# A kept value is joined into the last product's half bank before that product instead of after it, and the last step's stores use other queues

## The chip, the cores and the metric

The kernel runs on one core of a Trainium2 chip. The metric is the device time of one execution in microseconds; the kernel before takes 2274.68 us, the median of 3 runs (2274.32 to 2275.0).

Engines are named as in the profile: PE (TensorE; its weight loads are listed apart as PEld), DVE (VectorE), ACT (ScalarE), POOL (GpSimd) and SP (SyncE, which here only issues DMAs). PSUM is the memory that matmuls write to; it comes in banks of 512 fp32 columns on 128 partitions.

## What is computed

A causal depthwise convolution over the sequence, whose 7 taps are the softmax of a small weight table per head, and behind it a two-layer network without biases, all in fp32:

```python
# x: (8, 4096, 192), weight: (8, 7)
w = softmax(weight, axis=-1)
out = np.einsum('hk,bskhg->bshg', w, x_unf)     # 7 shifted copies of x, 24 channels a head
x = out.reshape(32768, 192)
h = x @ w_in                                    # (192, 2048)
g = h * (1.0 / (1.0 + np.exp(-1.702 * h)))
return g @ w_out                                # (2048, 192)
```

## The kernel before

**Tiling.** The work goes in 32 big steps (`N_BIG`) of 1024 tokens: 512 positions from each of two sequences. A step has a first half, `hidden` (called twice), which multiplies the convolved tokens by `w_in` and applies the activation, and a second half, `second`, which multiplies the result by `w_out` and stores the output. Both use fast matrix multiplication schemes that trade products for sums: the first on 21 products (`TERMS`), the second on 25 (`FORM_OF`). The first big step has its own code (`first_step`, `second_first`); `second` is called for steps 1 to 31. While a step runs, DVE, ACT and POOL also prepare the convolution of the step after the next.

**The second half.** Its order is written out by hand in the list `PLAN`, the same list for all 31 steps. Each entry is an operation:

- `main f s to first`: begin a product of weight form `f` with the sum `s` into value `to`; `first` tells whether it overwrites or adds to what is there.
- `go n`: issue `n` of the product's steps. A step is four matmuls of 128 rows by 32 columns side by side on the array, three for the main product (one for each 32 output columns) and one for a side product (`side f s to`), which goes to the last 32 partitions of another bank and is copied out by ACT (L1016) when it is complete. A main product is four steps.
- `join dst a op b`: `dst = a + b` or `a - b` on DVE (`add_up`: L391 for a plus, L393 for a minus), 96 partitions by 256 columns.
- `seed dst src sign`: an ACT copy (L1020), to keep a value or to put a start value into PSUM.
- `turn m n o src`: a DVE transpose (L908) of a finished value into the output tile `osbs`; `store n o`: its DMAs (L919).
- `sum`, `acc`, `tap`, `cross`: sums of the activated tokens on DVE or by an adding DMA from POOL, and pieces of the next step's convolution.

A value is named `p0` to `p5` or `k0` to `k11`. The `k` values lie in SBUF. The `p` values are halves of three PSUM banks:

```python
mains, sides = (bs[0], bx[0], by[0]), (bx[1], bs[1], by[1])
...
return mains[i // 2][0:n3, i % 2 * T : (i % 2 + 1) * T] if name[0] == "p" else kept(i)
```

So `p4` and `p5` are the two halves of the bank `by[0]`. The profile calls this bank "sums" in odd steps and "slot" in even ones, because the tiles change roles from step to step.

The part of the plan that the change touches (two stretches; between them stand products 4, 15 and 12):

```python
("join", "p2", "p4", "+", "k3"), ("main", 8, 8, "p1", 0, 0, 2), ("go", 1),
("join", "k8", "k9", "+", "k5"), ("tap",), ("go", 1), ("join", "k8", "k7", "-", "k8"),
("main", 4, 6, "p4", 0), ("go", 1), ("turn", 1, 0, 1, "k10"), ("go", 1),
...
("turn", 1, 0, 0, "k6"), ("store", 0, 0), ("main", 24, 19, "p5", 0), ("go", 2), ("final",),
("join", "k1", "p3", "-", "k3"), ("go", 1), ("join", "k2", "p2", "-", "k4"),
("turn", 0, 0, 1, "k1"), ("store", 0, 1), ("go", 1), ("turn", 0, 1, 1, "k2"), ("store", 1, 1),
("join", "k1", "p5", "+", "k5"), ("turn", 0, 1, 0, "k1"), ("join", "k8", "k8", "+", "k0"),
("turn", 1, 1, 0, "k8"), ("store", 1, 0),
```

Product 24 is the last of a step and adds into `p5`. After it, `p5 + k5` is put into `k1` and turned, and `k8 + k0` is put into `k8` and turned; `k0` is the last side product, which ACT copies out.

**Queues.** Every engine takes its instructions in the order in which the program issues them, and the waits between engines are semaphore counts that a framework puts in from the tiles that an instruction reads and writes. Stores of steps 1 to 30 go out on SP's queue once both halves of a sequence are turned (`out_store`, `stored`). In the last step each of the four quarters is stored as soon as it is turned, in three DMAs (one for each 64 output columns), which alternate between the queues of ACT and SP:

```python
queues = (nc.sync, nc.scalar) if o else (nc.scalar, nc.sync)
store(big, n, o, queues + queues[0:1])
```

Of the kernel before, what the change touches and what calls it, by code (L numbers as in the profile page):

```python
# [15 lines left out]
def kernel(  # L16
# [29 lines left out]
    nc = tc.nc  # L46
# [92 lines left out]
    def spot(i):  # L139

        if i >= SPOTS:
            return block(*divmod(i - SPOTS, NG))
        flat = osbs[:, i * BLK : (i + 1) * BLK] if i < 2 else room[:, ROOMS[i - 2], :]
        return flat.rearrange("p (k t) -> p k t", k=NG)
# [3 lines left out]
    def kept(i):  # L148

        if i < NG * len(KEPT):  # L150
            return room[0 : NC * Q, KEPT[i // NG], i % NG * T : (i % NG + 1) * T]
        return spot(KEPT_LATE)[0 : NC * Q, i % NG, :]
# [66 lines left out]
    def form(i):  # L219

        if i < WHOLE:
            return w_out_s[:, i // NG, i % NG * NG : (i % NG + 1) * NG, :]
        return w_form[:, i - WHOLE, :, :]
# [165 lines left out]
    def add_up(v, dst, a, op, b, eng=vec):  # L389
        if op == "+":  # L390
            eng.tensor_add(v(dst), v(a), v(b))  # L391
        elif op == "-":
            eng.tensor_sub(v(dst), v(a), v(b))  # L393
        elif op == "n":
            vec.scalar_tensor_tensor(
                out=v(dst), in0=v(a), scalar=-1.0, in1=v(b), op0=ALU.mult, op1=ALU.subtract
            )
        else:
            vec.tensor_scalar_mul(v(dst), v(a), -1.0)
# [164 lines left out]
    def cross_piece():  # L564
        if pieces:
            cross(*pieces.pop(0))
# [195 lines left out]
    def chunk_cols(c):  # L762
        return slice(c * Q, (c + 1) * Q)
# [136 lines left out]
    def blocks(t):  # L900
        return t.rearrange("p (j t) -> p j t", t=Q)

    def chunk(t, c):
        return t[c * Q : (c + 1) * Q]

    def turn(m, n, src, js):

        vec.transpose(osb[:, n, js, m * Q : (m + 1) * Q], src)  # L908


    def store(big, n, o=None, queues=(nc.sync,) * 3):
        p, c = divmod(big, CHUNKS)
        js = slice(0, TOK // Q) if o is None else slice(o * T // Q, (o + 1) * T // Q)
        t = c * TOK + js.start * Q
        rows = out_v[n, p, t : t + (js.stop - js.start) * Q, :].rearrange(
            "(j i) (c e) -> c i j e", i=Q, e=2 * Q
        )
        for c in range(NC):
            queues[c].dma_start(out=rows[c], in_=osb[c * Q : (c + 1) * Q, n, js, :])  # L919
# [27 lines left out]
        ("side", 7, 20, "k1"), ("go", 2), ("sum", 6, 6, "-", 17), ("main", 10, 14, "p0", 0), ("go", 2),  # L947
        ("seed", "k5", "p2", 1), ("tap",), ("cross",), ("join", "k10", "k10", "+", "k8"), ("go", 2),
        ("join", "p2", "p4", "+", "k3"), ("main", 8, 8, "p1", 0, 0, 2), ("go", 1),
        ("join", "k8", "k9", "+", "k5"), ("tap",), ("go", 1), ("join", "k8", "k7", "-", "k8"),  # L950
        ("main", 4, 6, "p4", 0), ("go", 1), ("turn", 1, 0, 1, "k10"), ("go", 1),
        ("join", "k3", "p1", "+", "k6"), ("go", 1), ("tap",), ("join", "k3", "p0", "-", "k3"), ("go", 1),
        ("join", "k6", "k0", "-", "p0"), ("side", 8, 5, "k0"), ("main", 15, 12, "p2", 0), ("go", 2),
# [3 lines left out]
        ("turn", 1, 0, 0, "k6"), ("store", 0, 0), ("main", 24, 19, "p5", 0), ("go", 2), ("final",),  # L957
        ("join", "k1", "p3", "-", "k3"), ("go", 1), ("join", "k2", "p2", "-", "k4"),
        ("turn", 0, 0, 1, "k1"), ("store", 0, 1), ("go", 1), ("turn", 0, 1, 1, "k2"), ("store", 1, 1),
        ("join", "k1", "p5", "+", "k5"), ("turn", 0, 1, 0, "k1"), ("join", "k8", "k8", "+", "k0"),  # L960
        ("turn", 1, 1, 0, "k8"), ("store", 1, 0),
    ]

    def sum_g(dst, a, op, b=None):

        if op == "acc":
            nc.gpsimd.dma_start(out=spot(dst), in_=spot(a), accum_op=ALU.add)  # L967
        else:
            add_up(spot, dst, a, op, b)

    SIDE_HALF = (0, 0, 1, 0, 1, 0, 1)

    def second(big, bx, by, bs, final, last):

        n3 = NC * Q
        mains, sides = (bs[0], bx[0], by[0]), (bx[1], bs[1], by[1])
        side, count = [], [0]
        now = {}  # L980
        stored = {0: 0, 1: 0}

        def value(name):
            i = int(name[1:])
            return mains[i // 2][0:n3, i % 2 * T : (i % 2 + 1) * T] if name[0] == "p" else kept(i)

        def product(f, s, k0=0, k1=NG):
            return [(form(FORM_OF[f])[:, k, :], spot(s)[:, k, :]) for k in range(k0, k1)]

        def one_matmul(dst, w, t, first, last):  # L990
            nc.tensor.matmul(dst, w, t, start=first, stop=last, skip_group_check=True)  # L991

        def begin_side(f, s, to, *ks):
            steps = product(f, s, *ks)
            for c in range(NC):
                turns, i = divmod(count[0], NC)
                h = SIDE_HALF[turns]
                count[0] += 1
                dst = sides[i][n3:, h * T : (h + 1) * T]
                for k, (w, t) in enumerate(steps):  # L1000
                    end = k == len(steps) - 1
                    side.append((dst, w[:, chunk_cols(c)], t, k == 0 and h == 0, end and chunk(value(to), c)))

        def begin_main(f, s, to, first, *ks):
            now.update(steps=product(f, s, *ks), to=value(to), first=bool(first))

        def go(n):
            for _ in range(n):
                w, t = now["steps"].pop(0)
                for c in range(NC):  # L1010
                    one_matmul(chunk(now["to"], c), w[:, chunk_cols(c)], t, now["first"], not now["steps"])
                now["first"] = False
                d, ws, ts, st, to = side.pop(0)
                one_matmul(d, ws, ts, st, to is not False)
                if to is not False:
                    act.copy(to, d)  # L1016

        def seed(dst, src, sign):
            if sign == 1:
                act.copy(value(dst), value(src))  # L1020
            else:
                act.mul(value(dst), value(src), -1.0)

        def out_turn(m, n, o, src):
            turn(m, n, blocks(value(src)), slice(o * T // Q, (o + 1) * T // Q))

        def out_store(n, o):
            if last:
                queues = (nc.sync, nc.scalar) if o else (nc.scalar, nc.sync)
                store(big, n, o, queues + queues[0:1])  # L1030
                return
            stored[n] += 1
            if stored[n] == 2:
                store(big, n)

        ops = dict(
            sum=sum_g, acc=lambda d, a: sum_g(d, a, "acc"), main=begin_main, side=begin_side, go=go, seed=seed,
            join=lambda d, a, op, b: add_up(value, d, a, op, b), turn=out_turn, store=out_store,
            tap=next_tap, cross=cross_piece, final=final,
        )  # L1040
        for item in PLAN:
            ops[item[0]](*item[1:])
        assert not side and not now["steps"] and count[0] == NC * len(SIDE_HALF)
        while pieces:
            cross_piece()
# [250 lines left out]
```

## Time and profile before

| | |
|---|---|
| median of 3 runs | 2274.68 us |
| the profiled execution | 2274.41 us |
| its span, first to last instruction | 2272.6 us |
| granted TensorE clock | 1.000 |
| PE busy | 2263.4 us |
| DVE busy | 1941.0 us |
| ACT busy | 1568.8 us |
| POOL busy | 847.0 us |

The span is what the trace covers; the 1.8 us between it and the execution's own time lie before the first and after the last instruction. Busy times are of one engine each and overlap. In a line of the timeline the first number is the start in us from the span's beginning, the second how long the instruction or the run of like instructions took; then come the engine, the line of the kernel, the operation, the tile written and those read, the shape, the count, and in brackets the idle time of that engine just before, with what ended it. A fp32 matmul is recorded as two passes, each with its weight load.

### The profile page before, as it was taken

How to read it: one execution, taken by the hardware profiler on the slowest of the kernel's cores; microseconds unless marked ns; L12 is line 12 of the kernel's file. 1: busy time of each engine (PE TensorE's matmuls, PEld its weight loads, DVE VectorE, ACT ScalarE, POOL GpSimd, SP SyncE). 2: the span in 40 equal slices, each digit the busy share in tenths (PEclk: the TensorE clock that was granted, in tenths of full speed). 3: DMA queues.
4: the chain of work that ended last, by engine and by line, in shares of the span. 5: the costliest groups of instructions: out<-in, count | busy, mean ns of one | idle time of the engine just before them, and what ended most of it. 6: DMA issues, size and time to landing. Idle time of an engine off the chain costs nothing.

```text
span 2272.6 us, 60950 instructions
## 1 busy us (share of the span) xinstructions
PE 2263.4 (100%) x25214; PEld 1214.9 (53%) x25214; DVE 1941.0 (85%) x2794; ACT 1568.8 (69%) x2972; POOL 847.0 (37%) x834
## 2 busy tenths in 40 slices
PE   9999999999999999999999999999999999999998
PEld 5475555555555555555555555555555555555556
DVE  8998888888888888888888888888888888888877
ACT  8866776667766667666677666776667766667754
POOL 1544443244442344433444324444244442344400
PEclk9999999999999999999999999999999999999999
DMA  9976656656566665666655675656666566664443
GB/s 205 155 146 127 127 111 126 137 122 131 116 126 129 123 139 114 116 126 134 134 120 109 126 144 121 131 112 127 132 126 136 112 124 126 129 139 86 88 99 71
DMA packets 269908, 284.20 MB, mean 125 GB/s; under 512 B 117952, under 2 KB 206016, under 8 KB 269632
## 3 DMA queue, kind: packets, MB, share of 16 engines
q0 software_dynamic: 57648, 150.69, 36.9%
q1 hardware_dynamic: 210336, 129.22, 25.2%
q8 instruction: 199, 3.26, 0.6%
q14 instruction: 77, 0.63, 0.1%
q10 hardware_dynamic: 1648, 0.39, 0.1%
HBM read 53.15 MB, written 25.17 MB: 34 GB/s over the span
## 4 chain that ended last, share of the span: by engine, by line
PE 99%; DVE 1%; ACT 0%; DMA 0%; issue 0%; SPq 0%; ACTq 0%; DVEq 0%
PE slot L616 35%; PE slot L991 33%; PE sums L616 16%; PE sums L991 13%; PE slot L822 2%; DMA xin<-in_x_dram 0%; DVE room L657 0%; DVE xt L473 0%; ACT conv_t L1096 0%; DVE conv_t L504 0%; SPq L99 0%; ACT conv_t L357 0%; DVE room L393 0%; ACT conv_t L356 0%; DVE g L391 0%
## 5 line engine op out<-in xcount | busy, mean ns | idle before, releaser
L616 PE MATMUL slot<-conv_t,w_in_s 64*128 64x512 f32 x3740 | 862.5, 591 | 0.3 <-DVE w_in_s L376 0.3
L991 PE MATMUL slot<-g,w_form 128*32 128x256 f32 x7024 | 710.8, 379 | 0.4 <-DVE room L657 0.4
L616 PEld LDWEIGHTS slot<-conv_t,w_in_s 64*128 64x128 f32 x3740 | 377.6, 187 | 423.9 <-issue 347.7
L393 DVE TENSOR_TENSOR g<-g 128x1024 f32<-128x1024 f32 x372 | 448.9, 1234 | 3.2
L991 PEld LDWEIGHTS slot<-g,w_form 128*32 128x32 f32 x7024 | 375.7, 110 | 118.1 <-DVE room L657 0.9
L616 PE MATMUL sums<-conv_t,w_in_s 64*128 64x512 f32 x1660 | 408.3, 589 | 0.3 <-DVE w_in_s L376 0.3
L1016 ACT COPY room<-slot 32x256 f32<-32x256 f32 x434 | 159.3, 367 | 310.3 <-PE slot L991 309.2
L642 ACT ACTIVATE g<-room 128x1024 f32<-128x1024 f32 x310 | 325.7, 1077 | 67.9 <-DVE room L657 67.9
L991 PE MATMUL sums<-g,w_form 128*32 128x256 f32 x2648 | 368.8, 379 | 0.0
L991 PE MATMUL slot<-g,w_out_s 128*32 128x256 f32 x4080 | 318.8, 380 | 0.0
L967 POOL DMA_DIRECT2D g<-g x124 | 106.2, 857 | 496.6 <-PE slot L991 156.8
L616 PEld LDWEIGHTS sums<-conv_t,w_in_s 64*128 64x128 f32 x1660 | 172.1, 187 | 184.9 <-issue 140.0
L518 POOL TENSOR_TENSOR conv_t<-conv_t,g 128x512 f32<-128x512 f32 x180 | 262.2, 1457 | 16.3 <-POOL conv_t L518 3.0
L530 POOL DMA_DIRECT2D g<-g x120 | 105.5, 879 | 422.5 <-PE sums L991 128.7
L653 ACT COPY room<-slot 128x512 f32<-128x512 f32 x434 | 231.4, 601 | 38.5 <-PE slot L616 38.4
L516 ACT ACTIVATE g<-xt,cw 128x512 f32<-128x512 f32 x360 | 248.5, 730 | 2.2
L991 PEld LDWEIGHTS slot<-g,w_out_s 128*32 128x32 f32 x4080 | 164.7, 110 | 128.5 <-ACT g L638 22.7
L638 ACT ACTIVATE g<-slot 128x512 f32<-128x512 f32 x334 | 180.8, 598 | 45.4 <-PE slot L616 24.8
L991 PEld LDWEIGHTS sums<-g,w_form 128*32 128x32 f32 x2648 | 177.9, 110 | 37.6
L504 DVE SCALAR_TENSOR_TENSOR conv_t<-xt,cw,conv_t 128x512 f32<-128x512 f32 (+1 forms) x198 | 192.0, 970 | 4.6
L393 POOL TENSOR_TENSOR conv_t<-conv_t 128x256 f32<-128x256 f32 x180 | 181.9, 1024 | 9.4
L1016 ACT COPY room<-sums 32x256 f32<-32x256 f32 x217 | 79.6, 367 | 145.0 <-PE sums L991 142.5
(205 smaller groups left out, 2909.5 us busy)
## 6 DMA issues: line engine op xcount, KB each, us to landing
g<-g POOLq DMA_DIRECT2D x124, 512.0 KB, 5.8
xin<-in_x_dram SPq DMA_DIRECT2D x240, 180.0 KB, 4.3
conv_t<-conv_t SPq DMA_DIRECT2D x180, 192.0 KB, 3.1
g<-g POOLq DMA_DIRECT2D x120, 256.0 KB, 3.8
out_dram<-osbs SPq DMA_DIRECT2D x186, 128.0 KB, 4.9
g<-room POOLq DMA_DIRECT2D x31, 512.0 KB, 5.3
conv_t<-g POOLq DMA_DIRECT2D x60, 256.0 KB, 4.8
g<-osbs POOLq DMA_DIRECT2D x30, 512.0 KB, 4.7
```

What stands on the lines that cost most here:

```text
L393: eng.tensor_sub(v(dst), v(a), v(b))
L504: vec.scalar_tensor_tensor(out=dst, in0=src, scalar=tap, in1=dst, op0=ALU.mult, op1=ALU.add)
L516: act.mul(home, conv_src(big, c, k), cw[:, c, k : k + 1])
L518: nc.gpsimd.tensor_add(dst, dst, home)
L530: nc.gpsimd.dma_start(out=out, in_=src, accum_op=ALU.add)
L616: nc.tensor.matmul(slot[h], w_in_s[halves[h], a, v * P : (v + 1) * P], src, start=first, stop=True, skip_group_check=True,)
L638: act.activation(dst[:, :, h, :], src[h].rearrange("p (o t) -> p o t", o=2), AF.Gelu_apprx_sigmoid)
L642: act.activation(dst.rearrange("p o h t -> p h o t"), src.rearrange("p h (o t) -> p h o t", o=2), AF.Gelu_apprx_sigmoid,)
L653: act.copy(bank(dst, h), bank(src, h))
L967: nc.gpsimd.dma_start(out=spot(dst), in_=spot(a), accum_op=ALU.add)
L991: nc.tensor.matmul(dst, w, t, start=first, stop=last, skip_group_check=True)
L1016: act.copy(to, d)
```

## The change

Three things are changed in the plan and the stores:

1. `p5 = p5 + k5` is done on DVE right after `k8 = k9 + k5`, ahead of products 4, 15, 12 and 24. Product 24 then adds onto the sum.
2. At the end of the plan the join `k1 = p5 + k5` is gone, and the transpose reads `p5` from PSUM.
3. In the last step the three DMAs of each quarter go to queues taken from a table: the first quarter as before (ACT, SP, ACT), the second SP, POOL, SP, the third POOL, SP, POOL, the fourth SP, ACT, SP.

The first two hold for all 31 steps that use the plan.

```diff
-        ("join", "k8", "k9", "+", "k5"), ("tap",), ("go", 1), ("join", "k8", "k7", "-", "k8"),
+        ("join", "k8", "k9", "+", "k5"), ("join", "p5", "p5", "+", "k5"), ("tap",), ("go", 1), ("join", "k8", "k7", "-", "k8"),
...
-        ("join", "k1", "p5", "+", "k5"), ("turn", 0, 1, 0, "k1"), ("join", "k8", "k8", "+", "k0"),
+        ("turn", 0, 1, 0, "p5"), ("join", "k8", "k8", "+", "k0"),
...
+    LAST_QUEUES = {
+        (0, 0): (nc.scalar, nc.sync, nc.scalar), (0, 1): (nc.sync, nc.gpsimd, nc.sync),
+        (1, 1): (nc.gpsimd, nc.sync, nc.gpsimd), (1, 0): (nc.sync, nc.scalar, nc.sync),
+    }
...
-                queues = (nc.sync, nc.scalar) if o else (nc.scalar, nc.sync)
-                store(big, n, o, queues + queues[0:1])
+                store(big, n, o, LAST_QUEUES[n, o])
```

## The prediction

> **What bounds the kernel now.** I read first the shares of busy time and the chain that ended last, on the page. PE is busy for the whole span, and the chain is PE from end to end; DVE has 1%.
>
> ```profile
> PE 2263.4 (100%) x25214; PEld 1214.9 (53%) x25214; DVE 1941.0 (85%) x2794; ACT 1568.8 (69%) x2972; POOL 847.0 (37%) x834
> ...
> PE 99%; DVE 1%; ACT 0%; DMA 0%; issue 0%; SPq 0%; ACTq 0%; DVEq 0%
> ```
>
> So work moved between DVE slots is free unless PE comes to wait for it, and whatever makes PE wait once in a step is paid 31 times. The question is therefore what PE waits for near the place where the join is put. I read that from the timeline of one step (big steps are 70.06 us apart: the same join starts at 2119.54 and, one step on, at 2189.60), by engine. First DVE, from 2119 us on:
>
> ```profile
> 2119.54 0.43 DVE L391 TENSOR_TENSOR slot<-sums,room 96x256 f32<-96x256 f32 x1 [1.75 <-ACT room L1020]
> 2119.88 0.41 DVE L391 TENSOR_TENSOR room<-room 96x256 f32<-96x256 f32 x1
> 2120.33 0.42 DVE L393 TENSOR_TENSOR room<-room 96x256 f32<-96x256 f32 x1
> 2120.67 0.43 DVE L908 STREAM_TRANSPOSE osbs<-room 96x256 f32<-96x256 f32 x1
> ```
>
> These are, in the plan's order, `p2 = p4 + k3`, `k8 = k9 + k5`, `k8 = k7 - k8` and `turn 1 0 1 k10`. DVE could not start sooner: it sat idle for 1.75 us until ACT had made `k5` (L1020). Now PE's weight loads and matmuls in the same stretch:
>
> ```profile
> 2120.02 0.12 PEld L991 LDWEIGHTS sums<-g,w_out_s 128*32 128x32 f32 x3 [0.15 <-DVE slot L391]
> 2120.04 0.11 PEld L991 LDWEIGHTS sums<-g,w_form 128*32 128x32 f32 x1
> 2120.17 0.12 PEld L991 LDWEIGHTS sums<-g,w_out_s 128*32 128x32 f32 x3
> ```
>
> ```profile
> 2120.17 0.39 PE L991 MATMUL sums<-g,w_out_s 128*32 128x256 f32 x3
> 2120.19 0.38 PE L991 MATMUL sums<-g,w_form 128*32 128x256 f32 x1
> 2120.39 0.39 PE L991 MATMUL sums<-g,w_out_s 128*32 128x256 f32 x3
> ```
>
> This is `main 4 6 p4`. Its first weight load waits for a DVE instruction of L391. The join into `p2` ends at 2119.54 + 0.43 = 2119.97, and the load starts 0.05 us later, at 2120.02. Its matmuls start at 2120.17, on the beat of 0.22 us of the sets before and after (2120.17, 2120.39). So this wait is already the last thing before `main 4`, and it costs nothing by a hair. The list of waits says that it is not one step's accident; the two rows differ by which bank `p4` lies in, odd or even steps:
>
> ```profile
> PEld sums L991 <- DVE slot L391: 2.4, 14, 0.4
> PEld slot L991 <- DVE slot L391: 2.1, 14, 0.2
> ```
>
> That is 28 steps of 31 with a wait of 0.15 us or so, hidden behind the matmuls still running.
>
> **The change part by part.**
>
> *The join of `k5` into `p5`, made earlier.* It goes between `k8 = k9 + k5` and `k8 = k7 - k8`, so it stands on DVE right behind 2119.88. Both operands are ready: `k5` was read by the instruction before it, and `p5` was last written by `main 23`, long over. Its result is accumulated onto by `main 24`, about 5 us later, which loses nothing. But `p5` is the second half of the bank whose first half is `p4` (`value`: bank `by[0]`, columns 256 to 511), and the built programs differ in one place that matters. In the program before, the load that opens `main 4 6 p4` waits until DVE's count is the one that `p2 = p4 + k3` raises (2698 in step 30). In the changed program it waits for 2700, the count that the new join raises. The wait goes by the bank, though `main 4` writes the other half.
>
> What that costs, from the rows above. DVE instructions that don't depend on each other start 0.34 us apart (2119.54 to 2119.88; 2120.33 to 2120.67). So `k8 = k9 + k5` stays at 2119.88 and the new join starts at 2120.22. It reads and writes PSUM; the nearest row is the join into `p2`, which does too: 0.43 (428 to 429 ns in all 31 steps). It ends at 2120.65, and the load that waits for it starts 0.05 later, at 2120.70 instead of 2120.02: **0.68 us later**.
>
> How much of this is still covered? The matmuls stood 0.15 us behind their load. The least they need is seen where PE truly stands still for a load, at the start of each step's second half:
>
> ```profile
> 2163.44 0.12 PEld L991 LDWEIGHTS slot<-g,w_out_s 128*32 128x32 f32 x3 [0.76 <-ACT g L638]
> ```
>
> ```profile
> 2163.44 0.42 PE L991 MATMUL slot<-g,w_out_s 128*32 128x256 f32 x3
> 2163.46 0.40 PE L991 MATMUL slot<-g,w_form 128*32 128x256 f32 x1
> 2163.68 0.39 PE L991 MATMUL slot<-g,w_out_s 128*32 128x256 f32 x3
> ```
>
> The second set comes 0.24 us after the load; a set takes 0.22; so the first one was really under way 0.02 to 0.03 us after its load started. The cover is 0.15 - 0.03 = 0.12, and the stall is 0.68 - 0.12 = **0.56 us a step**. The other end: if the load's recorded 0.11 us must pass first, the cover is 0.04 and the stall 0.64; with no cover at all it is 0.68. I take 0.56, from the row of the same shape in which PE does stand still. The Trainium skill ("TensorE: Matmul & The Clock Gate", section LDWEIGHTS) puts a weight load at its columns divided by 1.2 in ns, an estimate of 27 ns for the 32 columns here. By that the stall is the 0.56 already taken; by the recorded 0.11 us the sum would be 2.5 us more.
>
> Behind the waiting load stand all later matmuls; PE has no other queue. So all 31 calls pay it: 31 x 0.56 = **+17.4 us**. DVE's later work slips by less: `k8 = k7 - k8` moves from 2120.33 to 2120.56, and this is covered by the 0.91 us that DVE idles before `k1 = p3 - k3` at 2125.59, which moves with PE anyway.
>
> *The join taken out at the end, and the turn from PSUM.* Per step DVE keeps as many instructions. The turn waits for `main 24` where the join did, so after 2127.31 `p5` is read until 2127.75; the chain shows the first matmul into that bank in the next step at 2131.75, so 4 us of cover. Turning from PSUM took 0.69 against 0.66 from SBUF for 96x512 in the first step; nothing here. This pays only in the last step, whose end is on the path:
>
> ```profile
> 2266.57 0.42 DVE L391 TENSOR_TENSOR room<-sums,room 96x256 f32<-96x256 f32 x1 [0.29 <-PE sums L991]
> 2267.02 0.44 DVE L908 STREAM_TRANSPOSE osbs<-room 96x256 f32<-96x256 f32 x1
> 2267.84 0.42 DVE L391 TENSOR_TENSOR room<-room 96x256 f32<-96x256 f32 x1 [0.37 <-ACT room L1016]
> 2268.29 0.44 DVE L908 STREAM_TRANSPOSE osbs<-room 96x256 f32<-96x256 f32 x1
> ```
>
> Without the join the first turn runs 2266.57 to 2267.01. The next join waited 0.37 for an ACT copy, which stood behind a store that ACT was issuing until 2267.40; that store goes to POOL, so the copy runs at 2266.6 to 2267.0. Join and turn then take 2267.01 to 2267.90, and the last stores issue 0.83 us earlier than at 2268.76.
>
> *The stores.* ACT issues three instead of six, POOL three instead of none; SP still six. POOL's nearest row with two transfers per partition (2.42 us for two, at 91.98) gives 1.21 each. Three from 2265.97 on end at 2269.6, just where the last issue on ACT ends now (2269.18 + 0.46). So POOL may hand the 0.83 back. Bounds: -0.8 (POOL lands in time) to +1.1 (its landing takes 2.9 us after the issue, as 3.8 less 0.86 for 256 KB, against 1.8 on ACT). I take 0.
>
> **Sum.** The profiled execution took 2274.41 us, its span 2272.6 and 1.8 around it. 2274.4 + 17.4 + 0 = **2291.8 us**. The median of the runs is 2274.68, 0.3 above the profiled one; the range holds that.
>
> **Rivals.**
>
> *The wait costs PE nothing (not slower).* If the load needs only the join into `p2`, or if DVE reaches the new join 0.56 us sooner, `main 4` starts as now and only the tail is left: 2273.6 to 2274.4. For it: the two halves don't overlap, and today's wait is hidden. Against it: the count in the built program, and the 1.75 us for which DVE waits on ACT, which nothing in the change shortens. It decides at 0.12 us of added wait. The Trainium skill ("PSUM — Partial Sum Buffer", PSUM bank collisions raise a hardware error) says that waits on PSUM must go by bank and partition quadrant, not by address, since two engines in one bank collide even on different columns. By that rule the load has to wait for the join. No run here shows such a collision.
>
> *The stall is given back.* PE also pauses at the changes of stage: the set at 2163.44 comes 0.1 us off the beat, and about 0.2 goes at the step's start. If DVE and ACT used the added time to be early there, 0.3 would come back: 31 x 0.26 = 8, so 2282.5. Against it: both pauses follow DVE and ACT work that itself waited for PE in the same half (1.54 us idle on PE at 2159.32), so they move with PE.
>
> *No cover.* At 0.64 a step, 2294.3; at 0.68, 2295.5. If the new join also starts 0.45 behind its neighbour, as a dependent one does (2119.88 to 2120.33), 0.79 a step: 2299.
>
> **How the numbers follow.** Forecast 0.70; no cover 0.12; the latter with the longer spacing 0.04; given back 0.07; no cost 0.07. The range takes the forecast and the no-cover case: from 31 x 0.53 - 0.8 (2290, less 1 for a row read to 0.01 us) to 31 x 0.68 + 1.1 + 0.3 (2297). A measurement of this kernel tells 0.2% (4.5 us) from no change: slower 0.92, same 0.07, faster 0.01, since the tail alone is worth 0.04%.
>
> **What would show it.** In the changed profile: a third L391 instruction, out and in the same PSUM bank, about 0.34 us behind the second; the first weight load of `main 4` 0.05 us after its end, with an idle time near 0.8 instead of 0.15; a gap of 0.56 in PE's beat there, once a step, and steps 70.6 us apart. Wrong would be: steps still 70.06 apart, a load that starts before the new join ends, or gaps at the stage changes that shrink by as much. At the end, the last DVE turn should end 1.4 us after the last matmul instead of 2.2; three store issues on POOL near 1.2 us each.

## The result and the profile after

The changed kernel takes **2293.15 us**, the median of 6 runs (2292.69 to 2293.75); the kernel before takes 2274.37 (6 runs, 2273.59 to 2275.0). The ratio is 1.0083, with a 95% interval of 1.007 to 1.0096: slower by 18.8 us. The profiled execution took 2293.51 us, its span is 2291.6 (19.0 more than before). Forecast were 2291.8 us, in a range of 2289 to 2297.

The shares on the page, and the chain that ended last, of the changed kernel:

```profile
PE 2270.6 (99%) x25214; PEld 1209.1 (53%) x25214; DVE 1945.9 (85%) x2794; ACT 1568.7 (68%) x2972; POOL 846.5 (37%) x837
...
PE 96%; DVE 2%; ACT 1%; issue 0%; DMA 0%; SPq 0%; POOL 0%; POOLq 0%; ACTq 0%; DVEq 0%
```

The engines are as busy as before, but PE's part of the chain went from 99% to 96%, and DVE and ACT gained 1% each. The list of PE's waits says where; these two rows did not exist before:

```profile
PE sums L995 <- DVE sums L391: 5.6, 16, 0.6
PE slot L995 <- DVE slot L391: 5.1, 15, 0.3
```

16 + 15 waits, one in each of the 31 steps, on an L391 instruction that writes `p5`'s bank (`sums` in odd steps, `slot` in even ones). The first number is the total in us, the second how often, the third the longest. The total counts only the time in which PE's recorded matmuls left it idle, so it is less than what the steps lose. What a step loses is read from the timeline. DVE, from 2135 us on, one instruction a row (start, length, line, tile written and tiles read):

```profile
2135.16 0.43 DVE L391 TENSOR_TENSOR slot<-sums,room 96x256 f32<-96x256 f32 x1 [1.75 <-ACT room L1024]
2135.50 0.41 DVE L391 TENSOR_TENSOR room<-room 96x256 f32<-96x256 f32 x1
2135.83 0.42 DVE L391 TENSOR_TENSOR sums<-sums,room 96x256 f32<-96x256 f32 x1
2136.16 0.41 DVE L393 TENSOR_TENSOR room<-room 96x256 f32<-96x256 f32 x1
```

The third row is new: `p5 = p5 + k5`. The weight load and the matmuls of product 4 in the same stretch:

```profile
2136.30 0.12 PEld L995 LDWEIGHTS sums<-g,w_out_s 128*32 128x32 f32 x3 [0.82 <-DVE sums L391]
```

```profile
2135.35 0.61 PE L995 MATMUL slot<-g,w_form 128*32 128x256 f32 x8
2136.30 0.42 PE L995 MATMUL sums<-g,w_out_s 128*32 128x256 f32 x3 [0.34 <-DVE sums L391]
2136.32 0.40 PE L995 MATMUL sums<-g,w_form 128*32 128x256 f32 x1
2136.55 0.39 PE L995 MATMUL sums<-g,w_out_s 128*32 128x256 f32 x3
```

The join ends at 2135.83 + 0.42 = 2136.25; the load starts 0.05 later, 1.14 us behind the start of the join into `p2` (0.48 before). The second set of matmuls follows the load by 0.25 us; it was 0.24 where PE stood still in the kernel before. The same join into `p2` starts one step on at 2205.76, so a step takes 70.60 us; it took 70.06.

The end of the span. DVE's last instructions, POOL's stores, and the closing instructions of POOL and SP (for each kind: count, shortest, median and longest in ns, start of the first and the last):

```profile
2283.91 0.45 DVE L908 STREAM_TRANSPOSE osbs<-sums 96x256 f32<-96x256 f32 x1 [0.30 <-PE sums L995]
2284.34 0.42 DVE L391 TENSOR_TENSOR room<-room 96x256 f32<-96x256 f32 x1
2284.80 0.44 DVE L908 STREAM_TRANSPOSE osbs<-room 96x256 f32<-96x256 f32 x1
```

```profile
2283.58 1.82 POOL L919 DMA_DIRECT2D out_dram<-osbs  x3 [16.32 <-DVE osbs L908]
```

```profile
L1294 POOLq DRAIN  x3: 34/102/6301, 2284.5 to 2291.3; - x3
L1294 SPq DRAIN  x3: 7/7/7, 2288.5 to 2291.1; - x3
```

The same closing instructions in the kernel before:

```profile
L1291 POOLq DRAIN  x3: 39/102/8773, 2249.7 to 2272.3; - x3
L1291 SPq DRAIN  x3: 7/7/7, 2271.8 to 2272.1; - x3
```

DVE's last turn ends 1.33 us after it could first read `p5`; before, it was 2268.73 - 2266.57 = 2.16. SP has seen all its stores land by 2288.5. But POOL's first closing instruction, a drain that starts at 2284.5, lasts 6.30 us, to 2290.8, and the program ends behind it. Before, the same drain took 8.77 us from 2249.7 on, and was over long before the end.

From the start of the last matmul to the end of the span it is 8.1 us, against 6.3 before. So 19.0 = 31 x 0.545 (16.9) + 1.8 at the end + 0.3 from the stretch ahead of the first such join (it starts at 157.56 before and at 157.84 here). Nothing in that stretch was changed, and the start of this join differs by up to 0.9 us among the profiled executions of this document.

### The profile page after: what moved, and what is told of

Its sections match the earlier page's. It is cut to its first block, busy times and chain, and to the rows that moved or that the text cites. A ratio compares the mean times of both kernels' runs of the same rounds, so it can differ in the third digit from the quotient of the medians.

```text
span 2291.6 us, 60917 instructions
## 1 busy us (share of the span) xinstructions
PE 2270.6 (99%) x25214; PEld 1209.1 (53%) x25214; DVE 1945.9 (85%) x2794; ACT 1568.7 (68%) x2972; POOL 846.5 (37%) x837
## 4 chain that ended last, share of the span: by engine, by line
PE 96%; DVE 2%; ACT 1%; issue 0%; DMA 0%; SPq 0%; POOL 0%; POOLq 0%; ACTq 0%; DVEq 0%
PE slot L616 35%; PE slot L995 32%; PE sums L616 15%; PE sums L995 11%; PE slot L822 2%; DVE slot L391 1%; ACT room L1024 1%; ACT room L1020 0%; DVE room L391 0%; DVE sums L391 0%; DVE room L657 0%; DMA xin<-in_x_dram 0%; DVE xt L473 0%; ACT conv_t L1099 0%; DVE room L393 0%
## 5 line engine op out<-in xcount | busy, mean ns | idle before, releaser
L995 PEld LDWEIGHTS slot<-g,w_out_s 128*32 128x32 f32 x4080 | 163.3, 110 | 138.1 <-ACT g L638 22.7
```

## The experiments

The theory after this reading: PE waits in each step because product 4's load must wait for the last DVE instruction on its bank, and POOL's drain makes the rest. Times are medians against the kernel before on the same chip (2273.95, 2274.2 and 2273.98 us in the three groups). "Steps" is the distance of the same instruction from one big step to the next, "end" the time from the last matmul's start to the end of the span.

### The plan alone, and the queues alone

```diff
# plan alone: the diff without LAST_QUEUES
# queues alone: PLAN of before, with
+                store(big, n, o, LAST_QUEUES[n, o])
```

> The changed plan with the stores' queues of before. Theory (the wait on the bank costs 0.54 us in each of 31 steps, POOL's closing drain the other 1.8 us of the 18.8): a span of 2272.6 + 16.9 = 2289.5, steps 70.60 us apart, and an end like that of before, since the last ACT copy again stands behind a store on ACT's queue: some 1.8 us less than the changed kernel. Rival (the turn from PSUM or DVE's end of the step makes the last 1.8 us): the same span as the changed kernel, 2291.6.

Measured: 2290.74 us, ratio 1.0073 (1.0058 to 1.0088); steps 70.60, span 2288.6, end 5.6.

> The plan of before with the new queues for the last step's stores. Theory: steps stay 70.06 us apart; DVE's last turn ends 0.4 us sooner (the ACT copy is no longer behind a store, the join of p5 is still there), but POOL's closing drain ends some 5.4 us after POOL's last store was issued, and the span ends 1.7 us later than before: 2274.3. Rival (the new queues help, as the stores on SP are done 0.6 us sooner from the last matmul on): 2272.0 to 2272.2.

Measured: 2276.24 us, ratio 1.001 (1.0 to 1.0019); steps 70.06, end 7.7, span 2273.3 in the profiled execution, whose first steps came 0.6 us earlier than in before's. POOL's and SP's drains of the queues alone:

```profile
L1294 POOLq DRAIN  x3: 34/93/6015, 2266.6 to 2273.1; - x3
L1294 SPq DRAIN  x3: 7/7/7, 2270.3 to 2272.8; - x3
```

16.8 and 2.3 us: the parts add up to the whole, 18.8, within what the medians can tell. SP is done at 2270.3, 1.5 us sooner than before (0.9 sooner counted from the last matmul), and the span is not shorter, because POOL drains until 2266.6 + 6.0 = 2272.6. The plan alone has a better end than expected, 5.6 in place of 6.3: there the store ahead of the last ACT copy was issued in 0.38 us, where it took 1.42 before, and the copy was not late. Why the same issue took so different a time wasn't settled. The seven kernels here with the queues of before (the kernel before and those of the runs e1 and e3 to e7) end 5.6 to 6.3 us after the last matmul's start, so the share of the queues in the 18.8 us is known to some 0.7 us only: 8.1 - 6.3 = 1.8 against the kernel before, 8.1 - 5.6 = 2.5 against the plan alone.

### The join moved past product 4

```diff
-("join", "k8", "k9", "+", "k5"), ("join", "p5", "p5", "+", "k5"), ("tap",),
+("join", "k8", "k9", "+", "k5"), ("tap",),
...
-("join", "k7", "k4", "-", "p4"), ("go", 1),
+("join", "k7", "k4", "-", "p4"), ("join", "p5", "p5", "+", "k5"), ("go", 1),
```

> The queues of before; the early join of k5 into p5 stands behind the join k7 = k4 - p4, so after product 4 has finished with the other half of the bank, and ahead of product 24; the turn still reads PSUM. Theory (the place beside product 4 is the cost): no wait of PE's, steps 70.06 us apart, span 2272.6 +- 0.3. Rivals: if joining into PSUM, or turning from it, or one more DVE instruction ahead of the end of the step is what costs, the steps stay near 70.60 and the span near 2289.5; if half of it does, in between.

Measured: 2273.7 us, ratio 0.9999 (0.9989 to 1.0008); steps 70.06, span 2272.3. In its timeline:

```profile
2192.25 0.42 DVE L393 TENSOR_TENSOR room<-room,slot 96x256 f32<-96x256 f32 x1
2192.70 0.43 DVE L391 TENSOR_TENSOR slot<-slot,room 96x256 f32<-96x256 f32 x1
```

```profile
2190.14 0.12 PEld L991 LDWEIGHTS slot<-g,w_out_s 128*32 128x32 f32 x3 [0.15 <-DVE slot L391]
```

The join is the same instruction with the same 0.43 us (second row), it now stands behind the join `k7 = k4 - p4` (first row), and the turn reads PSUM as in the changed kernel; product 4's load again starts at once behind the join into `p2`. The whole step cost is the join's place.

### How the wait follows the join's end

Three kernels with the queues of before (swap, pad and read) move the end of the last DVE instruction on the bank, and one (dummy) puts an instruction there that has nothing to do with the bank. Swap and pad end as the changed plan does, with the turn from `p5`.

```diff
# swap
+("join", "p5", "p5", "+", "k5"), ("join", "k8", "k9", "+", "k5"), ("tap",),
# dummy: PLAN of before, with
+("join", "k8", "k9", "+", "k5"), ("join", "k9", "k9", "+", "k5"), ("tap",),
# pad
+("join", "k8", "k9", "+", "k5"), ("join", "k9", "k9", "+", "k5"), ("join", "p5", "p5", "+", "k5"), ("tap",),
# read: PLAN of before, with
+("join", "k8", "k9", "+", "k5"), ("join", "k5", "p5", "+", "k5"), ("tap",),
...
+("main", 24, 19, "p5", 1)
```

> The changed plan with the queues of before, and the new join one place earlier on DVE, ahead of k8 = k9 + k5. Theory: the load of product 4 waits for a join that ends 0.34 us sooner, 0.82 us behind the start of the join into p2 in place of 1.15; 0.12 us of the 0.34 that are added to before's 0.48 are covered, so the stall is 0.22 a step, the steps 70.28 apart, the span 2272.6 + 6.8 = 2279.4. Rival (the access to the bank slows PE, whatever is ahead of it on DVE): as e1, 2289.5.

Measured: 2284.38 us, ratio 1.0046 (1.0031 to 1.0061); steps 70.40 and span 2282.5, not 70.28 and 2279.4. The two joins of the swap, and the load behind them:

```profile
2199.51 0.89 DVE L391 TENSOR_TENSOR slot<-slot,room 96x256 f32<-96x256 f32 x2 [1.75 <-ACT room L1020]
```

```profile
2200.45 0.12 PEld L991 LDWEIGHTS slot<-g,w_out_s 128*32 128x32 f32 x3 [0.62 <-DVE slot L391]
```

The two take 0.89 us, so the second starts 0.46 behind the first and not 0.34 as an independent one would: it writes the bank that the first one reads, and in the trace it waits for the semaphore that DVE itself raises. The load comes 0.94 us behind the first join's start, not 0.82. The expectation had missed this; the rest of its rule holds, 0.94 - 0.48 - 0.12 = 0.34 a step.

> The kernel before with one more DVE instruction at the place of the new join, which touches no PSUM: k9 = k9 + k5, a value that nobody reads any more in the step (the computation is unchanged). Theory (PE waits for the bank, not for DVE being busy): product 4's load still starts 0.05 us after the join into p2, steps 70.06 us apart, span 2272.6 +- 0.5. Rival (DVE has no room there, and everything behind it in the step comes late): up to 0.45 us a step, 31 x 0.45 = 14 more.

Measured: 2273.85 us, ratio 0.9998 (0.9988 to 1.0009); steps 70.06, span 2272.4. The join into `p2` and the load:

```profile
2189.75 0.43 DVE L391 TENSOR_TENSOR slot<-slot,room 96x256 f32<-96x256 f32 x1 [1.75 <-ACT room L1020]
```

```profile
2190.23 0.12 PEld L991 LDWEIGHTS slot<-g,w_out_s 128*32 128x32 f32 x3
```

The load comes 0.48 us behind the start of the join, as in the kernel before, while the added instruction runs on DVE until 2190.96: PE waits for the bank and not for DVE, and DVE has the room.

> The changed plan with the queues of before, and the same harmless SBUF instruction put between k8 = k9 + k5 and the join into p5. It depends on the one before it, so it starts 0.45 behind it, and the join into p5 0.34 behind that: 1.13 us after the start of the join into p2, its end at 1.56, the load at 1.61. Theory: stall 1.61 - 0.48 - 0.12 = 1.01 a step, steps 71.07 apart, span near 2272.6 + 31.3 - 0.7 = 2303. Rival (a fixed cost of two engines in one bank): as e1, steps 70.60 and 2288.6.

Measured: 2304.99 us, ratio 1.0134 (1.0114 to 1.0154); steps 71.06, span 2302.8. The load, 1.60 us behind the start of the join into `p2` (expected: 1.61):

```profile
2220.16 0.12 PEld L991 LDWEIGHTS slot<-g,w_out_s 128*32 128x32 f32 x3 [1.27 <-DVE slot L391]
```

> The queues and the end of the plan of before, but p5 is only read at the early place (k5 = p5 + k5, into SBUF), and product 24 starts afresh in p5 instead of adding to it; the sum is made by the join at the end as before, so the result is the same. Theory (the wait goes by the bank, for a read as for a write): product 4 waits all the same. The instruction writes k5, which the one before it reads, so it starts 0.45 behind that one: load at 0.34 + 0.45 + 0.42 + 0.05 = 1.26, stall 0.66, steps 70.72 apart, span near 2293. Rival (only the write into PSUM holds PE up): 70.06 and 2272.6.

Measured: 2294.46 us, ratio 1.0088 (1.0068 to 1.0108); steps 70.71, span 2292.2. DVE's new instruction writes SBUF, and the load waits for it all the same:

```profile
2209.23 0.42 DVE L391 TENSOR_TENSOR room<-slot,room 96x256 f32<-96x256 f32 x1
```

```profile
2209.70 0.12 PEld L991 LDWEIGHTS slot<-g,w_out_s 128*32 128x32 f32 x3 [0.93 <-DVE room L391]
```

Put together, from the start of the join into `p2`:

| kernel | load starts after | later than before | step longer by | not paid |
|---|---|---|---|---|
| before | 0.48 | 0 | 0 | |
| swap | 0.94 | 0.46 | 0.34 | 0.12 |
| changed | 1.14 | 0.66 | 0.54 | 0.12 |
| read | 1.26 | 0.78 | 0.65 | 0.13 |
| pad | 1.60 | 1.12 | 1.00 | 0.12 |

The step grows by what the load is late, less the same 0.12 us, whether DVE writes or only reads the other half of the bank.

### The end: where POOL's stores stand, and no POOL at all

All three have the late join of e3.

```diff
# e9: LAST_QUEUES as changed
# e8
+        (0, 0): (nc.gpsimd, nc.sync, nc.gpsimd), (0, 1): (nc.sync, nc.scalar, nc.sync),
+        (1, 1): (nc.sync, nc.sync, nc.sync), (1, 0): (nc.sync, nc.scalar, nc.sync),
# e10
+        (0, 0): (nc.scalar, nc.sync, nc.scalar), (0, 1): (nc.sync, nc.sync, nc.sync),
+        (1, 1): (nc.sync, nc.sync, nc.sync), (1, 0): (nc.scalar, nc.sync, nc.scalar),
```

> The late join of e3, and POOL's stores moved to the first quarter (POOL, SP, POOL; then SP, ACT, SP; SP, SP, SP; SP, ACT, SP). Theory (the span's end waits for POOL's closing drain, which ends 5.1 to 5.4 us after POOL's last store was issued): POOL issues its last one some 0.5 us ahead of the last matmul in place of 1.9 us after it, its drain ends 5 us after the last matmul, beside the wait of SP for its own stores, and the span ends 5.6 to 6.0 us after the last matmul's start (8.1 in the changed kernel, 6.3 before): 2272.0 to 2272.4. Rival (the drain takes its 6 us from the last store of any queue, or POOL's stores land late however early): 8 us and 2274.3.

Measured: 2273.92 us, ratio 0.9998 (0.9988 to 1.0007); span 2272.7, end 6.25.

```profile
2264.84 1.24 POOL L919 DMA_DIRECT2D out_dram<-osbs  x2 [14.08 <-DVE osbs L908]
```

```profile
L1294 POOLq DRAIN  x3: 34/102/6607, 2265.3 to 2272.5; - x3
L1294 SPq DRAIN  x3: 7/7/7, 2271.5 to 2272.2; - x3
```

The drain goes with POOL's last store, and not with the last store of any queue: with that store issued earlier, the drain ends earlier too, at 2265.3 + 6.6 = 2271.9, and the end is 1.9 us shorter than in the changed kernel. But it still ends 0.4 us after SP's, and it lasts longer than expected: 5.9 us from the end of POOL's last issue, against 5.4 in the changed kernel and 5.1 with the queues alone.

The three agree when they are counted from the landing of POOL's last store. These rows of the list of DMAs are POOL's last store in the changed kernel (from 2284.9 us on), then in this one (from 2265.5 on), with its size and the us from issue to landing:

```profile
out_dram<-osbs POOLq DMA_DIRECT2D x1, 64.0 KB, 2.5
```

```profile
out_dram<-osbs POOLq DMA_DIRECT2D x1, 64.0 KB, 3.0
```

Issued at 2284.81, it landed at 2287.3 and the drain ended 3.5 us later, at 2290.8; here it was issued at 2265.47, landed at 2268.5, and the drain again ended 3.5 us later. With the queues alone, and in e9 below, it is 3.5 too. In the kernels where POOL's last transfer is an adding DMA of 512 KB, it is 3.4 (before: issued at 2249.70, landed 5.4 later, drain over at 2258.4). So the drain ends 3.4 to 3.5 us after POOL's own last transfer has landed, in all twelve kernels; what fills this time stays open.

> The changed kernel with only the join into p5 moved behind k7 = k4 - p4 (as in e3), the new queues kept. Theory (the two parts add up, and the whole step cost is the place of the join): steps 70.06 us apart, the end 7.7 to 8.1 us after the last matmul's start as in e2 and the changed kernel, so a span of 2274.0 to 2274.4 and 18 us less than the changed kernel. Rival (the queues or the turn from PSUM cost something in the steps as well): steps above 70.06.

Measured: 2275.89 us, ratio 1.0008 (0.9999 to 1.0017), 17.3 us below the changed kernel where 18 were expected; steps 70.06, end 7.9, span 2273.6 (its first steps came 0.6 us early). The parts add up: without the step cost, what is left is the end of the changed kernel.

> The late join of e3, and the second and third quarter's stores all on SP, none on POOL, the last quarter ACT, SP, ACT. Theory: the last ACT copy is no longer behind a store, so DVE's last turn ends 1.76 us after the start of the last matmul in place of 2.1 to 2.5, and without POOL's drain the span ends 5.6 us after it (6.3 before): 2271.9 +- 0.5, some 0.7 us below before, which the times alone can hardly show. Rival (SP, with seven stores ahead of its last one at 0.4 us each, is late by then): 6.0 to 6.3 and no gain.

Measured: 2274.45 us, ratio 1.0002 (0.9993 to 1.0011); end 6.1, span 2272.6. The rival holds: DVE's last turn ended at 2268.2, and SP issued the last store at 2269.2, since it worked off seven stores in a row from 2266.2 on. No version here beats the kernel before by more than can be measured.

## Why the prediction was right, and what it mis-sized

**The bound, and the wait that already stood at zero: right.** The load of product 4 started 0.05 us behind the last DVE instruction on the bank in every kernel, and the kernel that adds a DVE instruction but leaves the bank alone (e5) lost nothing.

**The new wait and its size: right.** Forecast were 0.68 us of delay, 0.12 of cover and 0.56 of stall; measured 0.66, 0.12 and 0.545. The missing 0.01 to 0.02 is that the new join starts 0.33 us behind its neighbour (forecast: 0.34) and takes 0.42 (forecast: 0.43). Every sign named for this came: the load 0.05 behind the join's end, its idle time at 0.82 (forecast: near 0.8), steps 70.60 us apart. 31 x 0.545 = 16.9, against 17.4.

**The cover: 0.12 held, and not 0.04.** The recorded 0.11 us of a weight load need not pass before its matmuls count as begun; the four kernels of the table that wait put the cover at 0.12 to 0.13. So 0.03 of the 0.15 us between load and matmul is not cover. This agrees with the prediction's estimate of 27 ns for the load, worked out from the Trainium skill, "TensorE: Matmul & The Clock Gate", section LDWEIGHTS; no trace shows what fills the 0.03.

**The waits by bank: right, for reads too.** e7 shows that reading the other half holds PE up as writing it does: the load idles 0.93 us there. The Trainium skill ("PSUM — Partial Sum Buffer", PSUM bank collisions raise a hardware error) demands such waits by bank of whoever sets them, for reads as for writes, and the waits in these traces agree. Each bank is one tile of this program, so the runs don't tell whether the framework goes by the bank or by the tile. What the chip would do without the wait wasn't tried.

**Nothing given back: right.** At the start of each step's second half the weight loads wait for ACT 30 times, 22.7 us in all, before and after alike; and no kernel's step grew by clearly less than its load's delay less 0.12.

**The end: mis-sized, and for a reason that was not in the sum.** The term was 0, between -0.8 and +1.1; measured +1.8. DVE's part came as worked out: the last turn ends 0.83 us sooner, counted from DVE's first read of `p5`. The step that failed is "three from 2265.97 on end at 2269.6, just where the last issue on ACT ends now": POOL issued a store in 0.6 us, not the forecast 1.2, and its last issue was over at 2285.4, 1.9 us after the start of the last matmul, where 3.3 were forecast (2269.6 - 2266.26). What came late was POOL's own closing drain, 5.4 us after its last issue, which the trace of before shows (8.77 us, from 2249.7 on) but which the prediction did not price, as it lay in no one's way there. So the sum came out 1.4 us low (17.4 against 18.8): 0.5 too much for the steps, 1.8 too little for the end. That it came no further off is in part luck, since the two errors have opposite signs and the end term lay outside its own bounds.

## What to carry to other kernels

Where two values share a PSUM bank and the waits go by the bank, an instruction on the one stands in the way of matmuls on the other, so put it where the bank has nothing to do: the same join, moved by one product, cost nothing instead of 17 us. A wait that ends just in time is invisible in the totals; find it as a short idle time with the same releaser in nearly every step, take the cover behind it from a place where the engine really stands still, and count what comes after that as paid in full. Before giving an engine its first late DMA, look at its closing drain, and at where it would then end: POOL's ended 3.4 to 3.5 us after its last transfer had landed, in every kernel here.

## What the runs showed that was not expected

- POOL's closing drain lasts 6.0 to 6.6 us when POOL has stored shortly before, and ends 3.5 us after its last store has landed, though SP had seen its own later stores land up to 2.4 us sooner. Behind the adding DMAs of the kernel before it lasts 8.5 to 8.9 us, and ends 3.4 us after the last of them has landed.
- POOL issues a store of 64 KB in 0.59 to 0.64 us; on SP and ACT the same issue took from 0.32 to 1.42 us, and why is open.
- DVE instructions on different halves of one bank are made to wait for each other as well: 0.46 us from start to start in e4, against 0.34 for independent ones.
